# Attention feeding a SwiGLU block on one core: k transposed by DMA straight into the score operands, and seven block products in token tile 1

## The chip, the core and the metric

The kernel runs on one core of a Trainium2 chip. A core has five engines, each with a queue of its own that is worked off in order: TensorE (PE in the profile, its weight loads PEld) multiplies matrices into PSUM; VectorE (DVE) and ScalarE (ACT) work element by element and read PSUM; GpSimd (POOL) does masks, casts and subtractions in SBUF and issues DMAs; SyncE (SP) only issues DMAs. All DMAs run on the core's 16 DMA engines. The metric is the device time of one execution in microseconds: a median of 376.06 over three runs before the change.

## The reference

Eight batches of eight heads, 576 positions, head width 64. The scores get a bias made of running sums of a gate `s`, a causal mask and a softmax; the heads' outputs, side by side, are the 4608 tokens of width 512 of a SwiGLU block of inner width 1536.

```python
scores = scale * np.matmul(q, k.transpose(0, 1, 3, 2))
cum = np.cumsum(np.maximum(s, 0.0), axis=-1)
bias = -(cum[:, :, :, None] - cum[:, :, None, :])
scores = np.where(causal, -1000000000.0, scores + np.minimum(bias, 0.0))
attn = softmax(scores)               # written out in the reference
x = heads_side_by_side(attn @ v)     # 4608 x 512
g = x @ w_gate
out = (g * sigmoid(g) * (x @ w_val)) @ w_out
```

## The kernel before

**Attention.** The 64 heads are worked off in 16 half-batches `hb` of four heads; head `bh` is step `bh % 4` of half-batch `bh // 4`. The operands of a half-batch's scores stand in `KQ[hb % 2][r]`, r = 0 for its first two heads (steps 0 and 1), r = 1 for the other two. One such tile has 128 partitions and two planes: plane 1 for k, plane 0 for q, each with the two heads' 576 positions side by side. In tile r the 64 partitions from 64 r hold the transposed k or q. In the other 64, four rows hold the running sums of `s` in two bf16 parts with constants that make the matmul add the bias, and the other 60 are zero. These four rows are written by `aug` (L178 to L186, line L183), four small DMAs a half-batch, one a head. Since the two halves of `KQ` alternate, half-batch hb overwrites what half-batch hb-2 used.

`score_piece(bh, ci)` (L341 on) does the four chunks of a head's scores: matmuls on L359, the exponential on ScalarE (L369), and for chunks 0 and 3 a causal select on POOL (L374, L379). `av_piece` (L396) multiplies with v one head later, `av_out` (L412, L413) normalizes on VectorE, `x_out` (L430) stores a pair of heads from POOL into a scratch tensor `xs`, and `x_in` (L437) brings them back transposed into `XT`, which holds the tokens of three token tiles with the width on the partitions.

**How k and q get transposed.** Half-batches 0 to 4 are transposed on TensorE. From `NPE = 5` on, k and q are cast to bf16 (`cast_one`), stored to DRAM scratch with the two head pairs interleaved (`scratch`, L260: tensors `ks` and `qs` of 1152 rows by 128 columns), and read back with a DMA transpose on SP (L270) into the staging tiles `pk` and `pq`, 128 by 1152: partitions 0 to 63 belong to r = 0, 64 to 127 to r = 1. `split` (L274, VectorE) copies each half of a staging tile to its place in `KQ[hb % 2][r]`: four copies a half-batch.

**The block.** The 4608 tokens are nine token tiles `tt` of 512. `gate_value` makes 12 blocks of 128 inner rows, each with a gate and a value product (L629, four matmuls of 512 columns), a tanh on ScalarE (L650) and two VectorE operations (L652, L663). The down projection has two forms. `down_plain` (L686): 48 matmuls of 512 columns. `down_seven`: the 512 tokens, the 1536 inner rows and the 512 outputs are halved into 2x2 blocks, and seven block products take the place of eight (L735: 84 matmuls of 256 columns). For that, sums of the halves of the inner result are made for each pair of blocks on VectorE (L670, L671) and a difference on POOL (L672; for the last pair on VectorE); the results are recombined on ScalarE (L784, L850), VectorE (L774, L794, L852) and POOL (L800); and five combinations of blocks of `w_out` are prepared once by `weight_op`: three sums into a tile of their own (L606, L608, L610), two differences in place (L615, L619), each in two parts. `FIRST7 = 2` is the first token tile with seven products: tiles 0 and 1 are plain, the weight sums are made in tile 1's down stage, the differences at tile 2's start.

**The order.** All instructions are put down in one order by hand. A generator `attn_items` walks the heads from 8 on, score piece by score piece; after each, `side` places the accompanying work by `(step, ci)`. The outer loop walks the block's items and, after each, pumps attention as far as a linear schedule says (`span`, 36 items for a plain tile and 34.5 for a seven-product tile). Splits go into a list, `later`, that `do_later` takes one by one every second item in tile 1, every fourth in other tiles and at every item of a down stage; what is left at the start of a half-batch is done there. PSUM's eight banks are handed out in the order of their release in this program order.

For a half-batch hb of 6 or more, with h the half-batch under way: the casts are at h = hb-2, steps 0 and 1; the scratch stores at step 2; both transposes at step 3, chunk 0; `aug` at h = hb-1, step 0, chunk 1, on the POOL queue; the splits of k and q at steps 0 and 1 (a step later for hb 5 to 7). Half-batches 5 and 6 have their stores and transposes somewhat later.

Of the kernel before, what the change touches and what calls it, by code (L numbers as in the profile page):

```python
# [13 lines left out]
BF16 = mybir.dt.bfloat16  # L14
# [5 lines left out]
def kernel(  # L20
# [11 lines left out]
    nc = tc.nc  # L32
    PSUM = bass.MemoryType.PSUM

    B, H, S, D = q.shape
# [7 lines left out]
    NR = HB // 2  # L43
# [66 lines left out]
    with tc.manual_schedule():  # L110
# [147 lines left out]
        def scratch(hb):  # L258
            for name, SC in (("k", KS), ("q", QS)):
                nc.sync.dma_start(  # L260
                    SC[hb].rearrange("(x j) c -> x (j c)", j=J),
                    cts[name, hb].rearrange("x j r d -> x (j r d)"),
                )

        prs = {}

        def transposes(hb):
            for name, SC in (("k", KS), ("q", QS)):
                prs[name, hb] = cp.tile([128, NR * S], BF16, tag="p" + name, bufs=1, name="p" + name)
                nc.sync.dma_start_transpose(prs[name, hb], SC[hb])  # L270

        def split(hb, name, r):
            kq = SRC[name][1]
            nc.vector.tensor_copy(  # L274
                KQ[hb % 2][r][64 * r : 64 * r + 64, kq, 0 : NR * S],
                prs[name, hb][64 * r : 64 * r + 64, :],
            )

        tps = {}
# [177 lines left out]
        def do_later(n):  # L457
            while n > 0 and later:
                f, *args = later.pop(0)
                f(*args)  # L460
                n -= 1
# [5 lines left out]
        def side(h, step, ci):  # L467
            bh = HB * h + step
            for c in V1_AT.get((bh, ci), ()):
                cast_v(1, c, nc.gpsimd)  # L470
            if bh == H + 4 and ci == 3:
                load_v(2, range(5))
            if h == 4 and (step, ci) in ((0, 1), (2, 1)):
                load_qk(6 + step // 2)
            if h >= 5 and h + 3 < NHB and (step, ci) == (0, 1):
                load_qk(h + 3)
            hb = h + 1
            if NPE <= hb < NHB:
                late = hb == NPE
                if late and (step, ci) == (0, 1):  # L480
                    scratch(hb)
                if late and (step, ci) == (0, 3):
                    transposes(hb)
                if (step, ci) == (0, 1):
                    aug(hb, GP4)
                first = 1 if hb < NPE + 3 else 0
                if step in (first, first + 1) and ci == (3 if late else 1):
                    for r in range(NR):
                        later.append((split, hb, "kq"[step - first], r))
            hb = h + 2  # L490
            if hb == NPE and step == 3 and ci % 2 == 1:
                cast_one(hb, "kq"[ci // 2], nc.gpsimd)
            if NPE < hb < NHB:
                six = hb == NPE + 1
                if (step, ci) == ((2, 0) if six else (0, 2)):
                    cast_one(hb, "k", nc.scalar)
                if (step, ci) == ((2, 2) if six else (1, 2)):
                    cast_one(hb, "q", nc.scalar)
                if (step, ci) == ((3, 0) if six else (2, 0)):
                    scratch(hb)  # L500
                if (step, ci) == (3, 3 if six else 0):
                    do_later(NR * 2)
                    transposes(hb)
            if ci != 1:
                return
            bn = h // 2 + 1
            if 3 <= bn < B:
                if h % 2 == 0:
                    if step == 2:
                        load_v(bn, (0, 1))  # L510
                    if step == 3:
                        load_v(bn, (2, 3, 4))
# [34 lines left out]
        def attn_items():  # L547
            for kk in range(H, BH + 2):
                h, step = divmod(kk, HB)
                if kk < BH:  # L550
                    if step == 0:
                        do_later(NR * 2)
                    if step == 1 and 3 < h + 1 < NPE:
                        cast_one(h + 1, "k", nc.gpsimd)
                        cast_one(h + 1, "q", nc.gpsimd)
                    if step == 2 and 3 < h + 1 < NPE:
                        aug(h + 1, GP4)
                    for ci in range(4):
                        score_piece(kk, ci)
                        side(h, step, ci)  # L560
                        side_v(h, step, ci)
                        yield kk + 0.1 + ci / 8
                        if (step, ci) in PREP_AT.get(h, ()):
                            prep_one(
                                h + 1, PREP_AT[h][step, ci],
                                (nc.scalar, nc.vector)[ci // 2] if h == 2 else None,
                            )
                            yield kk + 0.1 + ci / 8
# [17 lines left out]
                        yield kk + 0.8  # L586

        stores = []
        FIRST7 = 2
        HD = DM // 2  # L590
        HT = TT // 2
        NP = NFT // 2
# [394 lines left out]
                except StopIteration:  # L987
                    state["pos"] = 1e9

        W_SUMS = [(j, i) for i in range(3) for j in range(2)]  # L990
        W_DIFFS = [(j, i) for i in (3, 4) for j in range(2)]
        LAGS = [0, 1.65] + [3.6] * NTT
        hook = {n: [] for n in range(1, 37)}
# [71 lines left out]
```

## Time and profile before

| what | value |
|---|---|
| median of three runs | 376.06 us (374.64, 376.06, 376.85) |
| the profiled execution | 376.97 us, its span 375.3 us |
| granted TensorE clock | 0.994 |
| TensorE busy | 364.6 us, 97% |
| VectorE busy | 290.4 us, 77% |
| ScalarE busy | 240.6 us, 64% |
| POOL busy | 212.2 us, 57% |
| DMA | 64.23 MB, 171 GB/s on the mean |

Busy shares are means over stages with different limits, so the row of 40 slices (9.4 us each, a digit for tenths) and the busy time by stretch say more. A group's line gives the source line, engine, operation, output and inputs, shapes and count, then busy us and mean ns of one, then the engine's idle time before it and what ended it. A line of waits gives who waited for whom, the us in total, how often, and the longest.

Times of some places in the profiled execution, by the timeline: token tile 1 begins at 77.1 us (first gate product), tile 2 at 119.8, tile 3 at 158.9, then one each 39.1 us while attention lasts. Half-batches begin (first score matmul) at 86.77 (5), 104.29 (6), 120.97 (7), 141.09 (8), 160.03 (9), 180.14 (10), 199.08 (11), 219.20 (12), 238.14 (13), 258.26 (14) and 277.20 (15).

### The profile page before, as it was taken

To read this page: it belongs to the slowest core of one execution; us is meant where nothing else is said; L and a number is where in the kernel's file an instruction comes from. 1 tells how busy PE (TensorE), PEld (TensorE's weight loads), DVE (VectorE), ACT (ScalarE), POOL (GpSimd) and SP (SyncE) were. 2 spreads that over 40 slices of the span, in tenths; PEclk is the share of its full clock that TensorE was granted. 3 is DMA by queue.
4 is the path that set the end of the run, shared out by engine and by line. 5 is a ranking of instruction groups with operands and counts; after the bars stand their busy time and mean duration, and the time that the engine had idled before them with its cause. 6 is when DMAs were issued, how large, how long until landed. Compare 5 with 4: busy or idle time off the path is not lost.

```text
span 375.3 us, 8799 instructions
## 1 busy us (share of the span) xinstructions
PE 364.6 (97%) x3300; PEld 231.7 (62%) x3300; DVE 290.4 (77%) x578; ACT 240.6 (64%) x471; POOL 212.2 (57%) x325
## 2 busy tenths in 40 slices
PE   7799999999999999999999999999999999999995
PEld 6575556655555556855685558655865585476464
DVE  7777877458995999679976997599858867975984
ACT  8597687598976887578757876687465523323321
POOL 8973556765465647494649555955675416315320
PEclk9899999999999999999999999999999999999999
DMA  7899999899778986896769665995132103002003
GB/s 237 200 263 265 186 256 275 224 312 242 228 197 233 264 237 189 169 291 213 206 157 263 174 161 166 263 184 161 39 110 72 35 19 127 2 0 92 23 0 114
DMA packets 97147, 64.23 MB, mean 171 GB/s; under 512 B 77233, under 2 KB 82737, under 8 KB 97105
## 3 DMA queue, kind: packets, MB, share of 16 engines
q1 hardware_dynamic: 84976, 41.46, 45.3%
q0 software_dynamic: 12128, 22.21, 22.6%
q8 instruction: 26, 0.43, 0.5%
q14 instruction: 17, 0.13, 0.1%
HBM read 37.90 MB, written 19.86 MB: 154 GB/s over the span
## 4 chain that ended last, share of the span: by engine, by line
PE 90%; POOL 3%; DVE 2%; ACT 1%; DMA 1%; issue 1%; DVEq 0%; POOLq 0%; ACTq 0%
PE bank L629 47%; PE bank L735 17%; PE bank L359 11%; PE bank L396 8%; PE bank L686 6%; DMA kq<-HL 1%; ACT pt L369 1%; DVE kq L316 1%; DVE pp L652 1%; PE bank L287 1%; PE bank L353 1%; POOL vt L168 1%; PE bank L445 1%; DVE ht L663 1%; ACT th L650 0%
## 5 line engine op out<-in xcount | busy, mean ns | idle before, releaser
L369 ACT ACTIVATE pt<-bank 128x512 bf16<-128x512 f32 (+1 forms) x256 | 120.6, 508 | 31.5 <-PE bank L359 18.9
L629 PE MATMUL bank<-XT,wg 128*128 128x512 bf16 x432 | 111.4, 379 | 0.4 <-DVE pp L652 0.3
L629 PE MATMUL bank<-XT,wv 128*128 128x512 bf16 x432 | 110.9, 379 | 0.1
L650 ACT ACTIVATE th<-bank 128x512 bf16<-128x512 f32 x108 | 64.7, 599 | 56.1 <-PE bank L629 51.4
L652 DVE SCALAR_TENSOR_TENSOR pp<-th,bank 128x512 bf16<-128x512 bf16 x108 | 73.7, 682 | 18.7 <-ACT th L650 18.2
L663 DVE SCALAR_TENSOR_TENSOR ht<-pp,bank 128x512 bf16<-128x512 bf16 x108 | 74.1, 686 | 10.3
L359 PE MATMUL bank<-kq 128*128 128x128 bf16 (+4 forms) x576 | 76.9, 243 | 2.5 <-DMA kq<-HL 2.0
L672 POOL TENSOR_TENSOR ht<-ht 128x512 bf16<-128x512 bf16 x35 | 40.4, 1154 | 52.3 <-DVE su L670 52.2
L359 PEld LDWEIGHTS <-kq 128*128 128x128 bf16 x576 | 46.6, 99 | 33.5 <-issue 2.8
L629 PEld LDWEIGHTS <-wv 128*128 128x128 bf16 x432 | 38.3, 98 | 36.3 <-issue 0.2
L629 PEld LDWEIGHTS <-wg 128*128 128x128 bf16 x432 | 38.3, 98 | 34.2 <-issue 0.7
L374 POOL TENSOR_SCALAR_AFFINE_SELECT pt<-pt 128x512 bf16<-128x512 bf16 x56 | 36.8, 657 | 30.0 <-ACT pt L369 22.8
L396 PEld LDWEIGHTS <-pt 128*128 128x128 bf16 x960 | 41.8, 98 | 17.1
L396 PE MATMUL bank<-vt,pt 128*128 128x65 bf16 x960 | 46.7, 194 | 0.1
L430 POOL DMA_DIRECT2D xs<-ot x24 | 21.7, 904 | 30.2 <-DVE ot L413 27.8
L735 PEld LDWEIGHTS <-ht 128*128 128x128 bf16 x336 | 31.1, 98 | 4.3
L413 DVE TENSOR_TENSOR ot<-bank,rc 128x320 bf16<-128x320 f32 x64 | 31.5, 491 | 2.2
L183 POOL DMA_DIRECT2D kq<-HL x48 | 28.9, 605 | 0.0
L686 PE MATMUL bank<-wo,ht 128*128 128x512 bf16 x96 | 25.8, 379 | 0.0
L735 PEld LDWEIGHTS <-su 128*128 128x128 bf16 x252 | 23.5, 98 | 3.3
L379 POOL TENSOR_SCALAR_AFFINE_SELECT pt<-pt 128x64 bf16<-128x64 bf16 x56 | 14.8, 264 | 16.3 <-ACT pt L369 16.1
L800 POOL TENSOR_TENSOR ysb<-ysb 128x512 f32<-128x512 f32 x12 | 15.2, 1270 | 15.3 <-DVE ysb L794 15.3
(93 smaller groups left out, 387.2 us busy)
## 6 DMA issues: line engine op xcount, KB each, us to landing
out_dram<-ysb POOLq DMA_DIRECT2D x32, 256.0 KB, 4.0
rawv<-in_v_dram SPq DMA_DIRECT2D x28, 256.0 KB
rawk<-in_k_dram SPq DMA_DIRECT2D x12, 576.0 KB
rawq<-in_q_dram SPq DMA_DIRECT2D x12, 576.0 KB
xs<-ot POOLq DMA_DIRECT2D x24, 160.0 KB, 3.8
ks<-ck SPq DMA_DIRECT2D x11, 288.0 KB
qs<-cq SPq DMA_DIRECT2D x11, 288.0 KB
rawk<-in_k_dram POOLq DMA_DIRECT2D x3, 576.0 KB, 7.6
```

The lines of the kernel that those rows point to most:

```text
L359: nc.tensor.matmul(sc[:, o : o + w], T[:, 1, e * S + 128 * tj : e * S + 128 * (tj + 1)], T[:, 0, e * S + lo : e * S + hi], start=not maske ...
L369: nc.scalar.activation(pt[:, c0 : c0 + n], sc, AF.Exp, scale=0.125)
L374: nc.gpsimd.affine_select(pt[:, 1088:1600], pt[:, 1088:1600], pattern=[[0, 4], [1, 128]], compare_op=ALU.is_ge, fill=zreg, base=0, channel ...
L396: nc.tensor.matmul(av[:, bi * (D + 1) : (bi + 1) * (D + 1)], pt[:, c0 : c0 + 128], VT[b % 2][:, tj, h, :], start=(tj == 0), stop=(tj == bi),)
L413: nc.vector.tensor_mul(ot[:, :, e * D : (e + 1) * D], av3[:, :, 0:D], rc[:, :, None].to_broadcast([128, NCH, D]),)
L629: nc.tensor.matmul(view(bs, TT), w[:, c, f0 : f0 + 128], xt[:, c, :], start=(c == 0), stop=(c == 3),)
L650: nc.scalar.activation(th, pg, AF.Tanh, scale=0.5)
L652: nc.vector.scalar_tensor_tensor(pp, in0=th, scalar=1.0, in1=pg, op0=ALU.add, op1=ALU.mult)
L663: nc.vector.scalar_tensor_tensor(hp[:, 2 * k2 : 2 * k2 + 2, :].rearrange("p a n -> p (a n)"), in0=pp, scalar=0.5, in1=pv, op0=ALU.mult, op ...
L672: (nc.vector if ft == NFT - 1 else nc.gpsimd).tensor_sub(hp[:, 1:3, :], hp[:, 1:4:2, :], hp[:, 0:3:2, :])
L686: nc.tensor.matmul(view(pys[ts_], DM), hps[ft // 2][:, 2 * (ft % 2) + half, c0 : c0 + 128], WO[j][:, ft % WKO, :], start=(ft == 0), stop=( ...
L735: nc.tensor.matmul(ps, lhs(p), rhs(p), start=(first and p == 0), stop=(last and p == NP - 1), skip_group_check=True,)
```

## The change

k's DMA transpose no longer goes to a staging tile. It is issued twice, once for each r, from `ks` into the k plane of `KQ[hb % 2][r]`, all 128 partitions. In each tile 64 partitions then hold the wanted k, and the other 64, where only the four bias rows matter, hold the other pair's k; against the 60 zero rows of the q plane these add nothing. `aug` overwrites the four rows afterwards and so has to come later: it moves from step 0 to step 2 of the half-batch before. k's two transposes are issued at that half-batch's head (step 0, chunk 0; for half-batch 5 at chunk 3); q's stays at step 3 of h = hb-2, with its staging tile and two splits, now put on the list at step 1, chunk 1 (step 2, chunk 3 for half-batch 5). `FIRST7` becomes 1, so tile 1 uses the seven products; the weight sums move to tile 0's down stage, now in the order of the weight's parts, and the differences to tile 1's start. Tile 1's `span` is 34.5.

```diff
-        def transposes(hb):
-            for name, SC in (("k", KS), ("q", QS)):
-                prs[name, hb] = cp.tile([128, NR * S], BF16, tag="p" + name, bufs=1, name="p" + name)
-                nc.sync.dma_start_transpose(prs[name, hb], SC[hb])
-
-        def split(hb, name, r):
-            kq = SRC[name][1]
+        def transposes_k(hb):
+            for r in range(NR):
+                nc.sync.dma_start_transpose(KQ[hb % 2][r][:, 1, 0 : NR * S], KS[hb])
+
+        def transposes_q(hb):
+            prs[hb] = cp.tile([128, NR * S], BF16, tag="pq", bufs=1, name="pq")
+            nc.sync.dma_start_transpose(prs[hb], QS[hb])
+
+        def split(hb, r):
             nc.vector.tensor_copy(
-                KQ[hb % 2][r][64 * r : 64 * r + 64, kq, 0 : NR * S],
-                prs[name, hb][64 * r : 64 * r + 64, :],
+                KQ[hb % 2][r][64 * r : 64 * r + 64, 0, 0 : NR * S],
+                prs[hb][64 * r : 64 * r + 64, :],
             )
...
+                if (step, ci) == (0, 3 if late else 0):
+                    transposes_k(hb)
                 if late and (step, ci) == (0, 3):
-                    transposes(hb)
-                if (step, ci) == (0, 1):
+                    transposes_q(hb)
+                if (step, ci) == (2, 1):
                     aug(hb, GP4)
-                first = 1 if hb < NPE + 3 else 0
-                if step in (first, first + 1) and ci == (3 if late else 1):
+                if (step, ci) == ((2, 3) if late else (1, 1)):
                     for r in range(NR):
-                        later.append((split, hb, "kq"[step - first], r))
+                        later.append((split, hb, r))
...
                 if (step, ci) == (3, 3 if six else 0):
-                    do_later(NR * 2)
-                    transposes(hb)
+                    do_later(NR)
+                    transposes_q(hb)
...
                     if step == 0:
-                        do_later(NR * 2)
+                        do_later(NR)
...
-        FIRST7 = 2
+        FIRST7 = 1
...
-        W_SUMS = [(j, i) for i in range(3) for j in range(2)]
+        W_SUMS = [(j, i) for j in range(2) for i in range(3)]
```

## The prediction

> **What bounds the kernel now.** I read the page's shares first, then TensorE's waits, then busy time by stretch, then the single instructions around the places where the change acts.
>
> ```profile
> PE 364.6 (97%) x3300; PEld 231.7 (62%) x3300; DVE 290.4 (77%) x578; ACT 240.6 (64%) x471; POOL 212.2 (57%) x325
> PE   7799999999999999999999999999999999999995
> DMA  7899999899778986896769665995132103002003
> PE 90%; POOL 3%; DVE 2%; ACT 1%; DMA 1%; issue 1%; DVEq 0%; POOLq 0%; ACTq 0%
> ```
>
> TensorE (PE) is the bound: 97% busy, 90% of the chain that ended last. All its waits together, the smallest left out:
>
> ```profile
> PE bank L359 <- DMA kq<-HL: 2.0, 1, 2.0
> PE bank L883 <- POOL ident masks.py:199: 1.4, 1, 1.4
> PE bank L353 <- ACT pt L369: 0.9, 4, 0.3
> PE bank L629 <- DVE pp L652: 0.3, 1, 0.3
> ```
>
> By the timeline these lie in the first 40 us, where the change does nothing. From 60 us to the end one matmul starts as the last one's columns are through: four of 512 columns take 0.86 us, six of 256 take 0.66 us, in every stage. So nothing that only relieves another engine shortens the run, and every wait put before a matmul after 60 us lengthens it. The next limit is seen by stretch (columns: width, then busy us of PE, PEld, DVE, ACT, POOL; clock; DMA share):
>
> ```profile
> 80.00:104.00 24.00, 23.88 (x233) 13.87 (x231) 21.38 (x42) 20.39 (x40) 10.66 (x20) 1.00 0.98 248
> 124.00:148.00 24.00, 24.00 (x210) 13.67 (x209) 22.14 (x46) 19.81 (x40) 13.77 (x20) 1.00 0.94 240
> ```
>
> The first is the gate and value stage of token tile 1, the second of tile 2, which already has the seven products: there VectorE is 92% busy and TensorE still unhindered.
>
> **The change part by part.** The sum is made against the profiled execution: span 375.3 us, 376.97 with what lies around it, 0.91 over the median of 376.06.
>
> *Seven products in tile 1, TensorE.* Removed: 48 matmuls of 512 columns (L686), spaced 0.86/4 = 0.2155 us: 10.34 us. Added: 84 of 256 columns (L735), which a late tile shows without anything between them:
>
> ```profile
> 302.25 9.17 PE bank L735 x84
> ```
>
> 10.34 - 9.17 = 1.17 us saved. With the 0.12 us that TensorE lacks in 80 to 104 us, 1.3 us is the most that the change can gain, 0.35%.
>
> *The same, VectorE.* Rows used:
>
> ```profile
> L670 DVE TENSOR_TENSOR su<-ht 128x512 bf16<-128x512 bf16 x42 | 18.0, 429 | 1.5
> L671 DVE TENSOR_TENSOR su<-ht 128x256 bf16<-128x256 bf16 x42 | 11.9, 284 | 0.0
> L274 DVE COPY kq<-pk 64x1152 bf16<-64x1152 bf16 x22 | 14.1, 643 | 0.3
> ```
>
> In 80 to 104 us come five pairs of sums, 5 x (0.429 + 0.284) = 3.57 us, and one weight difference, 0.57 (L619). Four splits of k go, by the timeline 0.44 + 0.46 + 0.88 + 0.46 = 2.24. Net +1.9: 21.38 becomes 23.3 of 24, 97%. Is that covered? Between a product's sum (L663) and its factor lie some 0.1 us each that VectorE cannot fill, and the stage lives on PSUM banks coming free. One such hand-over in tile 1 now, by the program's bank numbers set beside the timeline: L413 frees a bank at 93.74 and the gate product that takes it starts at 93.97, 0.2 us later; the tightest in tile 2 are 0.2 too. VectorE at 23.3 of 24 would run up to 2 us behind its present order by the end of the stage, so TensorE must wait. If tile 2's 92% is its limit, 23.3/0.9225 = 25.2: 1.2 us lost. If it can run at 97%, nothing. I take 0.8, since tile 2 is the nearer row.
>
> The four weight differences move ahead of tile 1 and queue on VectorE behind the last plain product of tile 0; VectorE idles there (0.98 us busy from 76 to 80). The six weight sums (4.1 us) move into tile 0's down stage, 60 to 77 us, where VectorE has 8.4 busy of 17: 0, at most 0.5 if the last copies of half-batch 4's operands (done 69.6, needed 70.2) slip. In tile 1's down stage VectorE loses those sums and two k splits and gets 3.0 us of recombining (two each of L852, L774, L794): less than before, 0. ScalarE's four copies of 0.59 become two of 0.59 and two of 0.37. POOL gets five subtractions of 1.15 us and two of 1.27, as in tile 2.
>
> *k straight into the operands.* Eleven half-batches (5 to 15) lose two splits each, 14.1 us of VectorE: 0 for the end, since TensorE waits for none of it. They get one DMA transpose more each, 295 KB. From 138 to 140 us one runs alone at a DMA share of 0.65: 1.3 us of all 16 DMA engines a half-batch of 19.5 us, +7%, beside a share of 0.7 to 1.0. On SP two issues, 1.2 us each when quiet and 2.9 at worst, now stand ahead of the q and k loads and of the transposes into XT (L437). SP waits there anyway, 93.9 us in all for the xs stores; the loads are used a half-batch later, and the XT transpose of 151.6 us has until 158.9. 0, at most 0.3. q's transpose moves up. The new wait of k's transposes for the scores two half-batches back ends before SP is there.
>
> *The bias rows (`aug`) leave step 0 for step 2.* They overwrite rows that k's transposes fill, so they must come after. Four POOL DMAs of 0.6 us; landing:
>
> ```profile
> DMA to landing us min/median/max: 1.9/4.4/5.7
> ```
>
> The first must land before the next half-batch's first score. POOL around it now, in half-batch 10:
>
> ```profile
> 193.04 0.63 POOL L374 TENSOR_SCALAR_AFFINE_SELECT pt<-pt 128x512 bf16<-128x512 bf16 x1 [2.97 <-ACT pt L369]
> 194.14 0.24 POOL L379 TENSOR_SCALAR_AFFINE_SELECT pt<-pt 128x64 bf16<-128x64 bf16 x1 [0.46 <-ACT pt L369]
> 195.74 0.89 POOL L430 DMA_DIRECT2D xs<-ot  x1 [1.36 <-DVE ot L413]
> ```
>
> `aug` comes after this L374, at 193.7; half-batch 11 starts at 199.08. Budget 5.4 us; likewise 5.3 to 5.4 before half-batches 9, 13 and 15, over 8 before 10, 12 and 14. That L374 waits for ScalarE, which waits for VectorE behind four splits (189.2 to 190.9); with two gone it should come some 1 us earlier. Under heavy load the first landed 4.9 to 5.2 us after issue. So 0; at the worst landing, 5.7, it would be 0.3 each, and at the worst of that queue, 7.6 for an xs store, 2.2 each. Behind `aug` POOL holds L379 and the xs store 2.4 us longer; the values that need L379 run at the end of step 3, at about 198.
>
> Half-batch 6 is tighter: there POOL first does tile 1's new fourth subtraction, which waits for VectorE's sums of block 7. Today that block ends at 98.0 (L663); with 1.3 to 2 us of lag, 0.7 of sums and 1.15 of subtraction `aug` goes out at about 101.2 and lands, after 2.8 to 4.9, at 104.0 to 106.1. It is needed at 104.29, or 105.1 with the 0.8 us above. From 0 to 1.0; I take 0.2.
>
> *A rule beside the row.* The Trainium skill, "DMA: Bandwidth & Descriptors", on the path of a DMA, gives a fixed 2 us plus bytes over 436 GB/s. By it `aug` would land after 2 us, half-batch 6 would cost nothing, and the sum would be 0.2 us lower. The trace's median of 4.4 us disagrees, and I go by the trace.
>
> *A rule against the change.* The same page, on latency and other measured facts, gives a DMA transpose 261 GB/s where the middle dimension isn't contiguous. That is an estimate of 1.1 us for 295 KB, near the row's 1.3, and no obstacle.
>
> *Sum.* -1.17 + 0.8 + 0.2 = -0.2 us on 376.97; on the median 375.9.
>
> **The rivals.**
> - *The bias rows land late* (slower). Place: the first score of half-batches 6, 9, 11, 13 and 15. It decides once a landing passes 5.4 us, or `aug` goes out a microsecond later than I read. For it: 4.9 to 5.2 under load, one store of 7.6, a DMA share near 1. Against it: the relief of ScalarE's chain, and quiet landings of 2 to 3 us late in the run. At 6.5 us: 4 x 1.1 + 1.3 = 5.7 more than the sum: about 381; at 5.7 us, about 377.5.
> - *VectorE becomes tile 1's bound* (slower). If late sums also delay POOL's subtractions and the selects behind them, 1.2 becomes 2 to 3 us: 377 to 378.
> - *Nothing waits.* VectorE fits at 97% and every `aug` lands in time: the full 1.2 to 1.3 us: 374.8.
> - *k's part buys nothing.* That is in my sum: the 14.1 us of VectorE are off the path; only tile 1 uses any of it.
>
> **How the numbers follow.** The bound of 0.5% is 1.9 us, about what a measurement of this kernel can tell from no change; the three runs before spread by 2.2. Chances: the forecast 0.40 (its own range 375.0 to 376.9), nothing waits 0.20, late bias rows 0.28, VectorE 0.12. Faster by over 0.5% needs more than the 1.3 us the mechanism has, so it comes from the spread of the medians: 0.10 of the case without waits and 0.02 of the forecast. Slower: 0.26 of the late rows, 0.06 of VectorE, 0.02 of the forecast. The rest, 0.54, is within. The range goes from 374.0 (full gain and a favourable median) to 380.5 (landings of about 6.3 us); 0.08 lies above it and 0.08 below.
>
> **What would show it.** In the changed profile: L735's count up by 84 and no plain product in tile 1; VectorE 95% busy or more in tile 1's gate stage and waits of gate, value or score products for VectorE of 0.5 to 1.2 us there; landings of `aug` at least 5.3 us ahead of the first score, with TensorE waiting for `kq<-HL` only in half-batch 6; POOL not waiting for SP's transposes. Waits of TensorE for `kq<-HL` in 9, 11, 13 and 15 would prove me wrong upwards; no wait in tile 1 at all, downwards. L359 taking longer than its columns would be something I have not seen here.

## The result, and the profile after

The changed kernel takes 380.89 us (median of 6 runs, 380.18 to 381.94) against 376.0 us for the kernel before on the same chip: a ratio of 1.0123, 95% interval 1.0076 to 1.0171. It is slower by 1.2%, and 380.89 lies just above the predicted range. From here on a median is of all executions of a kernel, while a ratio leaves out the six slow ones among them.

Line numbers in the changed kernel are 2 to 3 higher: L632 is the gate and value product, L655 and L666 VectorE's two factors, L673 and L674 the sums, L675 POOL's subtraction, L415 the normalised output, L276 the split of q, L618 and L622 the weight differences, L689 the plain and L738 the seven-product down projection, L361 the scores, L376 and L381 the selects, L432 the store of xs, L439 the transposes into XT, L269 those of k.

The page, its shares, the clock in 40 slices and the chain that ended last:

```profile
PE 364.7 (96%) x3336; PEld 235.3 (62%) x3336; DVE 290.8 (77%) x575; ACT 240.5 (63%) x471; POOL 222.4 (59%) x332
PEclk9999999998999999999999999999999999999998
PE 81%; DVE 10%; POOL 2%; ACT 2%; issue 1%; DMA 1%; DVEq 0%; POOLq 0%; ACTq 0%
```

The matmuls went up by 36, as 84 for 48 should. VectorE holds 10% of the chain where it held 2%. The clock falls short in the slice from 85 to 95 us. TensorE's two longest waits on VectorE, neither there before:

```profile
PE bank L632 <- DVE ot L415: 2.3, 2, 2.1
PE bank L361 <- DVE ot L415: 0.8, 1, 0.8
```

The stretch around the longest (columns as in the prediction: width, busy us of PE, PEld, DVE, ACT, POOL; then clock, DMA share, GB/s):

```profile
84.00:86.00 2.00, 0.11 (x1) 0.10 (x1) 1.93 (x5) 0.82 (x3) 0.90 (x1) 1.00 0.94 245
86.00:88.00 2.00, 2.00 (x16) 1.05 (x15) 1.86 (x4) 0.60 (x1) 1.23 (x2) 0.71 0.83 264
88.00:90.00 2.00, 2.00 (x13) 1.16 (x12) 1.86 (x3) 0.09 (x1) 0.76 (x2) 0.50 1.04 282
```

TensorE stands idle for 2.06 us while VectorE is full, and from 86.85 to 90.26 us it runs at half clock: matmuls of 512 columns come 427 ns apart in place of 215. VectorE just then, and POOL beside it, from the timeline:

```profile
83.59 0.28 DVE L674 TENSOR_TENSOR su<-ht 128x256 bf16<-128x256 bf16 x1
83.79 1.42 DVE L276 COPY kq<-pq 64x1152 bf16<-64x1152 bf16 x1
...
85.35 0.49 DVE L415 TENSOR_TENSOR ot<-bank,rc 128x320 bf16<-128x320 f32 x1
83.75 1.15 POOL L675 TENSOR_TENSOR ht<-ht 128x512 bf16<-128x512 bf16 x1 [0.37 <-DVE su L673]
```

The split takes 1.42 us (its median is 0.457). The sums ahead of it released POOL's subtraction, and the split does not end before that has. TensorE's next gate product needs the bank that L415 frees behind it.

**The account.** A loss is the time from one matmul's start to the next, less its columns' time. In the profile of after, all losses over 0.22 us behind the head of half-batch 3 lie between 60 and 120 us: 0.92 at 66.0 (scores wait for an output behind the weight sums of tile 0's down stage), 0.24 at 81.0, 2.23 at 83.6, 1.66 by the half clock, and 0.27, 0.43, 0.45, 0.55 and 0.23 from 98.9 to 118.6: 7.0 us, all in waits for VectorE or, the half clock, behind one. The kernel before has 0.3 there. Less that and the 1.17 saved it is 5.5. From the head of half-batch 3 to the end the kernel before took 375.3 - 51.17 = 324.1 us and the changed one 378.9 - 49.39 = 329.5: 5.4 more. The spans differ by 3.6 only, since the profiled run of before lost 1.8 us more ahead of that: in both the first scores waited, 2.0 and 1.8 us, but only in the kernel before did half clock follow. The half clock need not be part of the median's loss: the one run of the changed kernel with a granted clock of 1.000 took 381.09 us, the five at 0.993 to 0.996 between 380.18 and 381.94.

At first sight only the seven products cost, since behind the start no landing of the bias rows made TensorE wait. The runs show otherwise.

### The profile page after: what moved, and what is told of

It reads as the page before. It is cut to its first block, busy times and chain, and to the rows that moved or that the text cites. A ratio compares the mean times of both kernels' runs of the same rounds, so it can differ in the third digit from the quotient of the medians.

```text
span 378.9 us, 8951 instructions
## 1 busy us (share of the span) xinstructions
PE 364.7 (96%) x3336; PEld 235.3 (62%) x3336; DVE 290.8 (77%) x575; ACT 240.5 (63%) x471; POOL 222.4 (59%) x332
## 3 DMA queue, kind: packets, MB, share of 16 engines
q1 hardware_dynamic: 98000, 44.71, 50.2%
## 4 chain that ended last, share of the span: by engine, by line
PE 81%; DVE 10%; POOL 2%; ACT 2%; issue 1%; DMA 1%; DVEq 0%; POOLq 0%; ACTq 0%
PE bank L632 44%; PE bank L738 18%; PE bank L361 9%; PE bank L398 7%; PE bank L689 2%; DVE pp L655 2%; DVE ht L666 2%; DVE kq L318 1%; ACT pt L371 1%; DMA kq<-HL 1%; DVE kq L276 1%; DVE ot L415 1%; POOL vt L168 1%; DVE su L674 1%; PE bank L355 1%
## 5 line engine op out<-in xcount | busy, mean ns | idle before, releaser
L632 PE MATMUL bank<-XT,wg 128*128 128x512 bf16 x432 | 111.7, 380 | 2.9 <-DVE ot L415 2.1
L632 PE MATMUL bank<-XT,wv 128*128 128x512 bf16 x432 | 111.7, 381 | 0.4 <-DVE ot L415 0.3
L655 DVE SCALAR_TENSOR_TENSOR pp<-th,bank 128x512 bf16<-128x512 bf16 x108 | 73.6, 682 | 20.4 <-ACT th L653 20.0
L666 DVE SCALAR_TENSOR_TENSOR ht<-pp,bank 128x512 bf16<-128x512 bf16 x108 | 74.1, 686 | 10.8 <-DVE pp L655 0.5
L361 PE MATMUL bank<-kq 128*128 128x128 bf16 (+4 forms) x576 | 76.1, 240 | 3.1 <-DMA kq<-HL 1.8
L675 POOL TENSOR_TENSOR ht<-ht 128x512 bf16<-128x512 bf16 x40 | 46.2, 1156 | 47.2 <-DVE su L673 42.1
L361 PEld LDWEIGHTS <-kq 128*128 128x128 bf16 x576 | 45.9, 98 | 31.9 <-issue 3.4
L632 PEld LDWEIGHTS <-wv 128*128 128x128 bf16 x432 | 38.7, 98 | 37.2 <-issue 1.2
L632 PEld LDWEIGHTS <-wg 128*128 128x128 bf16 x432 | 38.7, 98 | 37.0 <-issue 3.8
L376 POOL TENSOR_SCALAR_AFFINE_SELECT pt<-pt 128x512 bf16<-128x512 bf16 x56 | 36.5, 653 | 25.0 <-ACT pt L371 20.5
L738 PEld LDWEIGHTS <-ht 128*128 128x128 bf16 x384 | 35.5, 98 | 4.8
L432 POOL DMA_DIRECT2D xs<-ot x24 | 21.6, 902 | 28.3 <-DVE ot L415 28.2
L415 DVE TENSOR_TENSOR ot<-bank,rc 128x320 bf16<-128x320 f32 x64 | 31.4, 491 | 2.2
L738 PEld LDWEIGHTS <-su 128*128 128x128 bf16 x288 | 26.8, 98 | 3.9 <-issue 0.2
L803 POOL TENSOR_TENSOR ysb<-ysb 128x512 f32<-128x512 f32 x14 | 17.8, 1271 | 15.7 <-DVE ysb L797 15.2
L738 PE MATMUL bank<-WS,ht 128*128 128x256 bf16 x192 | 26.2, 273 | 0.0
L738 PE MATMUL bank<-wo,su 128*128 128x256 bf16 x192 | 25.0, 272 | 0.0
```

What stands on the lines that cost most here:

```text
L361: nc.tensor.matmul(sc[:, o : o + w], T[:, 1, e * S + 128 * tj : e * S + 128 * (tj + 1)], T[:, 0, e * S + lo : e * S + hi], start=not maske ...
L376: nc.gpsimd.affine_select(pt[:, 1088:1600], pt[:, 1088:1600], pattern=[[0, 4], [1, 128]], compare_op=ALU.is_ge, fill=zreg, base=0, channel ...
L415: nc.vector.tensor_mul(ot[:, :, e * D : (e + 1) * D], av3[:, :, 0:D], rc[:, :, None].to_broadcast([128, NCH, D]),)
L632: nc.tensor.matmul(view(bs, TT), w[:, c, f0 : f0 + 128], xt[:, c, :], start=(c == 0), stop=(c == 3),)
L655: nc.vector.scalar_tensor_tensor(pp, in0=th, scalar=1.0, in1=pg, op0=ALU.add, op1=ALU.mult)
L666: nc.vector.scalar_tensor_tensor(hp[:, 2 * k2 : 2 * k2 + 2, :].rearrange("p a n -> p (a n)"), in0=pp, scalar=0.5, in1=pv, op0=ALU.mult, op ...
```

## The experiments

### Each part alone

K's part and the later bias rows, the seven products from tile 2 on as before:

```diff
-        FIRST7 = 1
+        FIRST7 = 2
```

> The changed kernel with the seven products beginning with tile 2 again, as before: only k's transposes and the later bias rows remain of the change. Theory (VectorE at the head of tile 1 loses the time, k's part and the bias rows cost nothing): the time of before, 376.0 us, within 0.8, no matmul of 60 to 120 us that waits over 0.4 us for VectorE, and no stretch of half clock. Rival (the later bias rows, or the transposes beside the loads, cost the time): 378 to 381 us, waits of the first scores for kq.

Measured: 382.3 us (380.06 to 386.28), ratio 1.0149 [1.0086, 1.0211]. That is above the rival's 381, with the waits it names: k's part alone costs as much as the whole change. TensorE's waits (3.0 of the 4.3 us stand at the kernel's start, where nothing is changed), then what stood around two of them on POOL, PE and SP:

```profile
PE bank L361 <- DMA kq<-HL: 4.3, 3, 3.0
PE bank L632 <- DMA XT<-xs: 1.8, 1, 1.8
PE bank L398 <- DVE ot L415: 0.8, 3, 0.4
```

```profile
99.93 2.39 POOL L183 DMA_DIRECT2D kq<-HL  x4 [1.55 <-DMA kq<-ks]
106.22 0.40 PE L361 MATMUL bank<-kq 128*128 128x128 bf16 x4 [1.12 <-DMA kq<-HL]
115.43 0.57 SPq L140 DMA_DIRECT2D rawk<-in_k_dram  x1
...
116.66 3.87 SPq L439 DMA_TRANSPOSE XT<-xs  x2
124.37 0.38 PE L632 MATMUL bank<-XT,wg 128*128 128x512 bf16 x1 [1.78 <-DMA XT<-xs]
```

POOL stood 1.55 us for k's transposes before it could issue the bias rows, and these took 6.25 us to land; the scores of half-batch 6 started as they did. The transposes into XT now stand right behind two loads of 576 KB; the first gate product of tile 2 waited for them. The losses from 86 us on: 0.39, 1.29 (bias rows), 1.95 (XT), and 0.39, 0.59 and 0.32 at half-batches 8, 10 and 12, 4.9 in all; head of half-batch 3 to end is 380.8 - 51.70 = 329.1, 5.0 over before. In the last three, POOL's subtraction comes behind the four issues of the bias rows and then runs against a split of q (1.24 us at 141.12, 1.39 at 180.61, 1.12 at 220.25).

The seven products alone:

```diff
 (kernel before)
-        FIRST7 = 2
+        FIRST7 = 1
-        W_SUMS = [(j, i) for i in range(3) for j in range(2)]
+        W_SUMS = [(j, i) for j in range(2) for i in range(3)]
```

> The kernel before with the seven products already in tile 1 and the weight sums in the changed order, k's splits as they were. Theory: as the changed kernel or slower, 381 to 384 us, since VectorE in tile 1 has four k splits (2.2 us) more than there; TensorE waits over 2 us near 84 us and then runs at half clock for some 3 us. Rival (the loss is k's part or the bias rows): 375 us, the gain of 1.17 us whole.

Measured: 380.57 us (380.42 to 380.86), 1.0117 [1.0066, 1.0168].

```profile
PE bank L629 <- DVE ot L413: 2.5, 1, 2.5
PE bank L359 <- DVE ot L413: 1.1, 1, 1.1
```

The time is just under the theory's 381; the wait near 84 us and the half clock behind it (granted 0.59 and 0.56 from 86 to 90 us) came as it said. The half clock again doesn't show in the times: 380.42 us at a granted clock of 1.000 and 380.42 at 0.993. So each part alone costs about 5 us, and both together cost about 5 us. They are not added. The likely reason is that TensorE waits only once: in the changed kernel tile 1 runs late behind VectorE, half-batch 6 begins at 108.08, and its bias rows landed at 108.01; at half-batch 8 the margin is 0.35 us. A run below, in which tile 1 is faster, has the waits for these rows again.

### Where the weight operations stand

```diff
 (changed kernel, differences spread over tile 1)
-            if tt == FIRST7:
-                for _ in range(3):
-                    weight_op(*todo.pop(0))
...
-                if todo and (i >= 24 if tt < FIRST7 else i % 2 == 1):
+                if todo and (i >= 24 if tt < FIRST7 else i % 4 == 3):
```

> The changed kernel with the four weight differences spread, one each after items 3, 7, 11 and 15 of tile 1, in place of three ahead of it and one after item 1. Theory (three in-place differences in a row at the head of tile 1 hold VectorE for 3.4 us, and the 2.2 us wait at 83.6 us with the half clock behind it follow from that): the wait and the slow stretch go, 3.4 us less than the changed kernel, 377 to 378.5 us, if what is moved does not collect later in the tile. Rival (VectorE's total in tile 1 is what counts, wherever the differences stand): the wait moves, and the time stays within 1 us of the changed kernel's 380.9.

```diff
 (changed kernel, all ten by a list)
+        W_AT = {
+            0: {24: (0, 0), 26: (0, 1), 28: (0, 2), 32: (1, 0), 33: (1, 1),
+                34: (1, 2), 35: (0, 3), 37: (0, 4)},
+            1: {3: (1, 3), 7: (1, 4)},
+        }
...
```

> The changed kernel with the ten weight operations put where VectorE idled in the profile: three sums after items 24, 26 and 28 of tile 0, three after items 32 to 34, two differences after items 35 and 37, and the last two differences after items 3 and 7 of tile 1. Theory: the wait of 0.9 us at 66 us, that of 2.2 us at 83.6 us and the half clock behind it go: 4.3 us less than the changed kernel, about 376.6 us (375.8 to 377.6); the small waits of 98 to 106 us (1.7 us) stay. Rival (VectorE's total is what counts): no more than 1 us less than the changed kernel.

Measured: 383.57 us, 1.0203 [1.0151, 1.0256], and 381.92, 1.0156 [1.0095, 1.0217]. Both theories missed; the second time fits the rival, the first is worse than either allowed. The waits of 2.39 us at 83.4 and 82.3 us stayed, and the first of the two kernels got a second one (its line of waits):

```profile
PE bank L632 <- DVE ot L415: 4.6, 3, 2.2
```

So it was not the number of differences in a row. Items 3 and 7, where I had put them, are those that end a pair of blocks: the difference came right behind the sums, beside the subtraction that these release. In the second kernel it took 1.53 us (82.16 to 83.69; POOL's L675 ran from 82.12 to 83.27), where one alone takes 0.57. That gave a new theory, collisions:

```diff
 (changed kernel; both of the last differences ahead of tile 1)
+            1: {-1: [(1, 3), (1, 4)]},
...
-                elif i >= 2 * NFT or i % (2 if tt == 1 else 4) == 1:
+                elif i >= 2 * NFT or i % 4 == 1:
                     do_later(1)
```

> The changed kernel with nothing but PSUM reads behind a pair of sums in tile 1: six sums and two differences after items 24 to 37 of tile 0, two differences ahead of tile 1, and the splits of q in tile 1 after items 1, 5, 9 as in the later tiles, in place of 1, 3, 5. New theory (VectorE's operations with both operands in SBUF, behind the sums, run against the GpSimd subtraction that these sums release, and are held until it ends: 0.57 becomes 1.53 us, 0.45 becomes 1.33): the wait of 2.2 to 2.4 us at 82 to 84 us falls under 0.7, the half clock behind it goes, no difference takes over 0.8 us in tile 1, and the time falls to 377 to 379 us; what is left are landings of the bias rows and of the transposes into XT that the slower tile had hidden, up to 3 us. Rival (VectorE's sum of work in tile 1 is too long, wherever it stands): the waits move to later in the tile, and the time stays at 380 us or over.

The same placing with k as before:

> The seven products alone (k's splits and the bias rows as before) with the same placing as in the run without collisions. New theory: the loss of the seven products alone, 7.5 us against a gain of 1.17, came from the collisions, so it falls to 1.5 us or less: 374 to 376.5 us, the time of before or up to 1 us under it. Rival (VectorE has 2.2 us more of k splits in tile 1 than the changed kernel, and is the bound): over 378 us.

The first of the two is the changed kernel with the list, its last two differences and its splits moved; the second has `FIRST7 = 1` and the same edit in the kernel before. Measured: 381.31 us, 1.0171 [1.0138, 1.0205], for the changed kernel, and 376.68, 1.0054 [1.0039, 1.0069], for the seven products alone. In both, the wait at 82 us fell to 0.57 and the half clock went. The seven products alone lost 5.6 us of median by collisions and order before (380.57 against 375.0) and 1.9 now (376.68 against 374.76). Its forecast of 376.5 at most was missed by 0.2. That all of it was collisions doesn't follow, since the edit moved more than them. By the traces 1.6 us of losses went at 63 to 67 us, where the weight sums of tile 0 had stood ahead of outputs and operands, 2.1 of the wait at 83 us and 1.7 of half clock behind it, and 1.8 came new, some 4 net. The collision itself is 0.9 us of the 2.1 (the split took 1.33 us beside POOL's subtraction, 0.46 alone); the rest, the order of VectorE's queue, the two runs don't part from it. For the changed kernel the forecast of 377 to 379 fell, and the time is in the rival's range. But what waits is not VectorE with too much work: of the landings that the slower tile had hidden came 4.6 us, more than the 3 allowed for (0.96 and 1.51 for the bias rows of half-batches 5 and 6, and 2.12 at 96.5 us). Nor is this kernel wholly free of collisions: the smaller sum took 1.89 us at 92.63, beside POOL's select and subtraction. Its waits (1.1 of the 3.2 at the start):

```profile
PE bank L361 <- DMA kq<-HL: 3.2, 3, 1.3
PE bank L398 <- DVE pp L655: 2.0, 1, 2.0
PE bank L632 <- DVE ot L415: 0.9, 3, 0.4
```

The 2.0 is VectorE's by name only: VectorE stood 1.6 us in front of a split of q whose transpose landed at 97.49, with a factor queued behind it.

### What of k's part costs

The bias rows in step 2, k's transposes and splits as before:

```diff
-                if (step, ci) == (0, 1):
+                if (step, ci) == (2, 1):
                     aug(hb, GP4)
```

> The kernel before with only the bias rows issued in step 2 in place of step 0; k's transposes and splits as they were. Theory A (the bias rows cost most of what k's part costs alone): a wait for kq at the head of half-batch 6 of 0.5 us or more, GpSimd's subtraction held behind the four issues at half-batches 8, 10 and 12 with a split of q over 1 us there and 0.3 to 0.6 us of TensorE waiting for the normalised output, and 1.5 to 3 us over before. Theory B (the second transpose of k on SP and the DMA engines costs it): the time of before within 0.8 us. In both the wait of 1.9 us for XT at the head of tile 2 is gone if k's transposes on SP's queue cause it.

Measured: 375.3 us, 1.0016 [1.0005, 1.0027], 0.5 us over before. Landings just reach the first scores (0.05 us of margin at half-batches 7, 9 and 11), with no wait for them over 0.2 us. That is theory B by the time; but TensorE waited 0.63 us for XT here as well, without k's transposes, its own transposes again close behind the two loads.

One more transpose of k, into a tile that nobody reads:

```diff
 (kernel before)
+                if (step, ci) == (0, 3 if late else 0):
+                    pd = cp.tile([128, NR * S], BF16, tag="pd", bufs=1, name="pd")
+                    nc.sync.dma_start_transpose(pd, KS[hb])
```

> The kernel before with one more DMA transpose of k a half-batch, at the head of the preceding half-batch, into a tile that nobody reads; k's own transpose, its splits and the bias rows as before. So SP and the DMA engines carry what they carry in the changed kernel, and nothing waits for the added transpose but the queue. Theory A (the load alone costs): a wait of 1 to 2 us for XT at the head of tile 2, landings of the later transposes behind it, and 1.5 us or more over before. Theory B (only the chain costs in which the bias rows stand behind k's transposes and the first scores behind the bias rows): no wait for kq, and within 0.8 us of before.

Measured: 380.04 us (376.77 to 385.62, a wide spread), 1.0126 [1.0086, 1.0165]. The load alone costs nearly what k's part does: theory A. The profile is of the fastest run, 2 us over before, and has one long wait, which is that much; what the median loses beyond it stands in no trace:

```profile
PE bank L632 <- DMA XT<-xs: 1.9, 1, 1.9
```

SP's queue ahead of it, in the kernel before and here:

```profile
108.55 0.57 SPq L140 DMA_DIRECT2D rawk<-in_k_dram  x1
...
114.75 2.40 SPq L437 DMA_TRANSPOSE XT<-xs  x2
```

```profile
110.34 1.30 SPq L484 DMA_TRANSPOSE pd<-ks  x1
111.70 0.58 SPq L140 DMA_DIRECT2D rawk<-in_k_dram  x1
...
113.01 3.34 SPq L437 DMA_TRANSPOSE XT<-xs  x2
```

Before, 5 us lay between the loads and XT's transposes. The added transpose pushed the loads up against these: issued at about the same place of the program (1.7 us earlier by the time, in a run that reached half-batch 3 2.1 us earlier), they landed only at 120.4, 2 us after tile 2's first gate product wanted them.

So I moved the loads, in k's part alone and in the changed kernel without collisions:

```diff
-            if h >= 5 and h + 3 < NHB and (step, ci) == (0, 1):
+            if h >= 5 and h + 3 < NHB and (step, ci) == (2, 0):
                 load_qk(h + 3)
```

> K's part alone, with the loads of q and k for the half-batch three ahead (two of 576 KB) issued at the head of step 2 in place of step 0, that is behind the bias rows' predecessors and the transposes into XT and no longer straight ahead of them. Theory (k's transposes push SP back, so that these loads meet the bias rows and the transposes into XT on the DMA engines): the waits of 1.3 us for kq at 105 us and of 1.9 us for XT at 122 us fall under 0.5 us each, the first landings of the bias rows take 4 us or less, and the time falls to 376 to 378.5 us. Rival (the transposes' own time on the DMA engines is the cause, wherever the loads stand): 380 us or over.

> The changed kernel without collisions and with the loads of q and k at the head of step 2. Theory (two independent causes: collisions on VectorE, and the DMA engines' queue): the waits for kq of 1.0 and 1.5 us and the 2.1 us at 96.5 us (a split that stood waiting for q's transpose ahead of a first factor) go, VectorE's 1.4 us stay, and 1.2 us of matmuls are saved: 375 to 377 us, about the time of before. Rival (either cause is not the one named): 379 us or over.

Measured: 385.29 us, 1.0254 [1.0222, 1.0287], and 384.65, 1.0239 [1.0204, 1.0274]. Both are in the range of their rivals, and slower than with the loads where they were. The wait for XT at tile 2's head went, but others came, of the first kernel (2.0 of the 3.3 at the start):

```profile
PE bank L361 <- DMA kq<-HL: 3.3, 3, 2.0
PE bank L398 <- POOL pt L381: 2.9, 4, 1.0
PE bank L361 <- DVE pp L655: 2.5, 2, 1.5
```

Now the loads went out beside the bias rows (140.14 and 140.25 us), and POOL, which stood 3.82 and 4.17 us for k's transposes before it could issue these, was late with selects. In neither place tried do the loads meet nobody, and the runs do not show whether a third would do.

Last, k's part only where the DMA engines are less full, from half-batch 9 on:

```diff
+        DIRECT = 9
...
+                if hb >= DIRECT and (step, ci) == (0, 0):
+                    transposes_k(hb)
+                if (step, ci) == ((2, 1) if hb >= DIRECT else (0, 1)):
                     aug(hb, GP4)
...
```

> K's part alone, and only for half-batches 9 to 15; 5 to 8 as before (k's splits, bias rows in step 0). K's part alone from half-batch 5 on cost 5 us or more, with waits at 105, 122, 143, 182 and 222 us in its profile. Theory A (it costs where the DMA engines are full, 60 to 145 us, tiles 1 and 2): those before 145 us go, what is left are the short waits at half-batches 10 and 12, 0.3 to 0.6 us each, and the time is 375 to 376.5 us. Theory B (it costs wherever the bias rows stand behind k's transposes, or by its SP issues): over half of the loss stays, 377.5 us or more.

Measured: 375.41 us, 1.0005 [0.9984, 1.0026]: theory A, no change at all, with 7 of the 11 half-batches converted. The one wait for bias rows left, 0.6 us, stands at the start of the kernel, where nothing is changed. K's part costs in half-batches 5 to 8 alone, and buys nothing in the others.

### The seven products further

Without collisions the seven products alone still lost 0.57, 1.13, 0.70 and 0.39 us in tile 1; 2.8 less 1.17 is 1.6, near the 1.9 measured. Four attempts at that rest, all on the kernel before with the placing without collisions.

The sums of a pair held back behind the next block's first factor:

```diff
-                if k2 == 1 and tt >= FIRST7:
+                if k2 == 1 and tt == FIRST7 and ft < NFT - 1:
+                    held.append(sums)        # called behind the next block's L652
...
```

> As the seven products without collisions (k as before), and in tile 1 each pair's sums are held back behind the next block's first factor, two splits go after item 1 and one after items 3, 7, 11. The waits left in that run were 0.57 us at 82.1 and 0.70 at 88.6 (normalised output queued behind a pair of sums of 0.72) and 1.13 at 84.8 (the splits of half-batch 5 queued behind two factors). Theory (VectorE's order, not its sum, makes them): they fall under 0.4 us together, and the time goes to 373.6 to 375 us, at or under the time of before. Rival (the order only moves them): 376 us or over.

Two splits after item 1:

```diff
-                    do_later(1)
+                    do_later(2 if tt == 1 and i == 1 else 1)
```

> The seven products without collisions, k as before, with two splits in place of one after item 1 of tile 1, where VectorE idled 0.36 us before the next factor. If VectorE's order makes the 1.13 us wait at the head of half-batch 5 (a third split of 0.45 stood ahead of it): the wait falls to 0.5 to 0.8 and the time from 376.7 to 375.8 to 376.4 us, still not under before's. If the order only moves waits within a full VectorE: 376.5 us or over.

K's splits of half-batches 5 and 6 on POOL:

```diff
-            nc.vector.tensor_copy(
+            (nc.gpsimd if name == "k" and hb < 7 else nc.vector).tensor_copy(
```

> The seven products without collisions, k as before, with the two splits of k of half-batches 5 and 6 done by GpSimd in place of VectorE (2.2 us less on VectorE in tile 1, no transpose added). Theory (VectorE's sum of work at the head of tile 1 makes the 2.8 us of waits left without collisions): they fall to 1.3 us or less and the time from 376.7 to 374.5 to 375.7, the time of before or just under. Rival (GpSimd's in-order queue takes VectorE's place: the splits hold its selects, or run against VectorE's copies and sums): 376.5 us or over.

And a longer lag at tile 1's start:

```diff
-        LAGS = [0, 1.65] + [3.6] * NTT
+        LAGS = [0, 2.3] + [3.6] * NTT      (and 3.0)
```

> The seven products without collisions, k as before, with the lag of the attention at the start of tile 1 at 2.3 score steps in place of 1.65, so that 0.65 steps more of the attention run beside tile 0 and as much less beside tile 1 (from tile 2 on the lag is 3.6, so tile 1 carries 9.95 steps where the later tiles carry 8). Theory (tile 1 has too much on VectorE since it carries two steps of attention more than the later tiles, which have the same seven products and no wait): the 2.8 us of waits in tile 1 fall to 2 or less, the time to 375.3 to 376.3 us. Rival (waits come from how the normalised outputs fall behind the sums, which any lag only shifts): 376.5 us or over, waits of 2.5 us or more.

> The same with a lag of 3.0 score steps. Theory: waits in tile 1 under 1.2 us, the time 374 to 375.5 us, at or under the time of before, if tile 0 can take 1.35 steps more without waits for half-batch 4's operands. Rival: new waits in tile 0, 376.5 us or over.

| edit | us | ratio to before |
|---|---|---|
| without collisions | 376.68 | 1.0054 [1.0039, 1.0069] |
| sums held back | 380.18 | 1.0124 [1.0080, 1.0168] |
| two splits first | 377.03 | 1.0052 [1.0025, 1.0079] |
| k's splits on POOL | 376.8 | 1.0050 [1.0020, 1.0080] |
| lag 2.3 | 379.98 | 1.0145 [1.0104, 1.0185] |
| lag 3.0 | 379.63 | 1.0123 [1.0101, 1.0144] |

Each time is in the rival's range. With two splits first, the 1.13 became 0.65, and the 0.57 ahead of it 0.73. With k's splits on POOL, tile 1's waits still sum to 2.75 (0.57, 0.64, 0.42, 1.12). That does not clear VectorE's sum of work, since the splits on POOL held VectorE up in their turn:

```profile
83.75 2.21 DVE L274 COPY kq<-pq 64x1152 bf16<-64x1152 bf16 x2
84.38 1.26 POOL L274 COPY kq<-pk 64x1152 bf16<-64x1152 bf16 x1
```

Q's two splits took 2.21 us, where without k's beside them they took 0.94, and from 76 to 102 us VectorE was busy 21.96 us against 23.15: 1.2 us less, not 2.2. In the kernel without collisions two of the four waits (0.57 and 0.70) have one picture, shown by VectorE's timeline:

```profile
81.39 0.42 DVE L670 TENSOR_TENSOR su<-ht 128x512 bf16<-128x512 bf16 x1
...
82.15 0.49 DVE L413 TENSOR_TENSOR ot<-bank,rc 128x320 bf16<-128x320 f32 x1
```

The pair of sums (0.7 us in all) stands ahead of the output whose bank the next gate product takes, at 82.70. The 1.13 is for a split ahead of half-batch 5's first scores, the 0.39 for a second factor. With a longer lag the scores of half-batch 5 come before its operands (a wait of 2.5 us for a split at 83.5 with lag 2.3; with lag 3.0 one of 0.8 for a cast of v at 77.4, and of 1.7 for a factor at 102.5), and both waits have a long split ahead of them, 1.33 us at 84.33 and 2.30 at 101.01. So neither run tests the lag by itself. Why tiles 2 to 6 carry the same products without a wait stays open; what was tried of amount, order and phase didn't show it. No version beat the kernel before.

## Why the prediction was wrong

It said 375.9 and named four small terms; two of them were wrong by several microseconds.

- *TensorE's gain, 1.17 us*: right. The matmuls changed as said, and the account closes with it.
- *VectorE in tile 1, 0.8 us (0 to 1.2)*: that TensorE would wait there for banks that VectorE frees late was right; the size was wrong, and so was what makes VectorE late. Without collisions and with k as before the loss is 2.8 us; in the changed kernel 6.1 us of the losses lie in tile 1 (4.4 of waiting, 1.7 of half clock). The step that failed is the transfer of a stage total, "23.3 of 24", to a loss: tile 2's 92% held no wait and was no guide to tile 1's. Nor was VectorE 95% busy there, the sign named for it:

```profile
80.00:104.00 24.00, 21.21 (x187) 12.04 (x185) 21.55 (x39) 16.15 (x33) 13.16 (x21) 0.93 0.90 238
```

In this window of the prediction's row TensorE was idle for 2.8 us, and VectorE itself for 2.45. It mattered what stood ahead of the output whose bank was wanted, and how long it was held. The durations failed too, since each was taken from a row in which the operation mostly runs alone: a split is 0.46 or 1.42, a difference 0.57 or 1.53. One of the prediction's own four splits, the 0.88, was such a case: it ran at 95.05, beside POOL's select of 94.97.

- *The weight differences queue where VectorE idles, 0*: wrong. The first three took 1.16, 0.98 and 1.23 us from 76.6 on, beside POOL's casts and selects, and the first factor of tile 1 started at 79.74, 3.6 us after its gate product began; before it was 79.47 against 77.05, 2.4 us.
- *The weight sums in tile 0, at most 0.5*: 0.92, for the output ahead of half-batch 4.
- *K's part, 0 (at most 0.3)*: the step that failed. That the 14.1 us of splits are off the path was right (with direct transposes from half-batch 9 on nothing changes). That another transpose is free was wrong: k's part alone costs 1.5%. By the profile's page the hardware queue's DMAs took 45.3% of 375.3 us and take 50.2% of 378.9: 20.2 us more over 11 half-batches, 1.8 us each, not 1.3. More important, I checked one transpose into XT, that of 151.6 us with 7 us to spare; the tight one was that of 114.75, for tile 2. In the trace of k's part alone that wait is 1.9 us of 4.9, beside 1.3 for the bias rows of half-batch 6. How much the added transpose costs by itself stays open: the run with nothing else lost 5 us by its median and 2 in its trace.

```profile
q1 hardware_dynamic: 84976, 41.46, 45.3%
q1 hardware_dynamic: 98000, 44.71, 50.2%
```

- *The bias rows*: 0 for half-batches 9, 11, 13 and 15 was right, and the rows landed 2.1 to 4.9 us ahead. The tight places were others than foretold: 10 and 12, given over 8 us, had 7.8 and 7.2 between issue and first score, of which landings of 6.7 and 5.7 us left 1.08 and 1.54, and 8, which was not named, kept 0.35. For 6 the 0.2 was luck: they went out at 103.96, not 101.2, landed after 4.05 us, and were in time only because tile 1 was late. Where it wasn't, landings took 6.25 us (k's part alone) and 5.13 (without collisions), beyond the 2.8 to 4.9 I allowed, and cost 1.3 and 1.5. The rival "late bias rows" named 381 us, and the time came out there, by another mechanism.
- *The sum*: terms were added as if independent. Alone they are some 5 us each, together some 5 us, since, as the margins suggest, a wait in tile 1 hides the late landings behind it. The account of one profile names the wait that came first, not all that are there.

## What to carry to other kernels

Before adding an operation to a full VectorE, ask what runs on GpSimd at that moment: here an operation with all its operands in SBUF, placed behind the instruction that releases a GpSimd operation, was held for about 1 us. Before adding a DMA, look for the tightest later transfer in the same queue, not for a typical one, and ask what it will then stand behind. When one profile shows a single cause, run each part alone: here the second cause was as large, and hidden.

## What the runs showed of the hardware

**VectorE and GpSimd hold each other up.** In the changed kernel the split takes 442 ns at the least, 457 at the median and 1422 beside POOL's L675; the weight difference 551 to 1228, and 1.53 us in the run with the list. The other way round, two of POOL's casts of v took 1.00 and 0.95 us beside the differences at 77 to 80 us, and 0.60 to 0.64 elsewhere. L655, with one operand in PSUM, took 659 to 689 ns in all 108 cases. The Trainium skill, "SBUF — State Buffer", section "SBUF: two separate sides", says that the port pair of the two engines is an exclusive lock held for the whole instruction, for a VectorE operation in a two-port mode or with two SBUF inputs against a GpSimd operation that reads SBUF. These numbers agree.

**A wait of 2 us can bring 3.4 us of half clock.** It came with idle times of TensorE of 2.02 (start of the kernel before), 2.06 (the changed kernel at 84 us), 2.22 (the list of weight operations), 2.30 (the changed kernel without collisions and with the loads moved, at 105 us), 2.48 (lag 2.3), 2.52 (seven products alone) and 2.97 us (k's part alone, start). After 2.22 and 2.14 (spread differences), 2.01 (k's part with the loads moved, start) and all idle times under 2.0 it did not. By the clock records of the traces it lasted 3.41 us each time, and began between 0.3 us ahead of the first matmul behind the wait and 1.3 us after it. The stretches at full clock ahead of it and between are whole multiples of the same 3.41 us: 6.83 us in the kernel before, 81.92 and 286.72 in the changed one. The Trainium skill, "TensorE: Matmul & The Clock Gate", section on the HAM clock gate, gives at least one idle window of about 3.4 us as the condition, free-running. Here 2.0 us were enough; that equal idle times went both ways, and the multiples of 3.41 us, fit a window that isn't bound to the program.
